# Attention's product with v does two or three steps in some slots and none in their neighbours

## The chip, the core and the metric

The kernel runs on one core of a Trainium2 chip. The core has five engines that take their instructions in order, each from its own list: TensorE (PE: matrix products and transposes, with PEld for the loads of its stationary operand), VectorE (DVE), ScalarE (ACT), GpSimd (POOL) and SyncE (SP, which issues the DMA transfers). They wait for one another on semaphores. The metric is the device time of one execution in microseconds (us).

## What is computed

Three stages follow one another, all on inputs in fp32 (the weights of the second arrive as 64-bit numbers):

```
q_assign = argmax(q_n . c_n); k_assign = argmax(k_n . c_n)     # 16 clusters
scores = where(q_assign == k_assign, q k^T / sqrt(64), -1e9)
attn = softmax(scores);  x = attn v                            # 2 x 8 heads, 768 rows, 64 wide
h = x w_in;  g = P(h) / Q(h);  x = g w_out                     # 1536 x 512, 2048 wide
out = soft mixture of 8 experts with 4 slots each (phi, w1, w2)
```

The change lies in the last product of attention, attn v.

## The kernel before

**Attention** works on pairs of heads: 8 pairs, and each pair in two halves of 384 query rows, so 16 half pairs. A half pair has 6 slots, one for each of 3 blocks of 128 query rows and 2 heads; there are 96 slots in all (NSL). The loop at L673 records slot after slot, and in this stage PE, ACT, DVE and POOL keep the order in which they are recorded (a manual schedule; SP too up to slot 12). In slot n:

- PE turns the exponentials of slot n, six transposes of 128x128 into the PSUM tile sT (`turn`, L413); ACT copies them out to eT (`turned`, L419).
- PE makes the scores of slot n+2: four products into the PSUM tile s (`a1_mm`, L389 and L390). DVE copies them out negated with their row minimum (`a1_neg`, L398, with a short instruction behind it that reads the minimum), and one slot later ACT takes the exponential (`a1_exp`, L402).
- PE does one step of the product with v of the half pair before (`a2_av`, L426). A half pair's product has six steps, one for each block j of 128 keys, summed up in the PSUM tile av; a step has a product for each of the two heads, which lie in two column halves of the array. One product of the kernel is two rows in the profile.
- Other work is planned into slots by name. On PE these are products with the centroids (L242), transposes (L263, L290, L447, L586, L607), products that make the masks (L312, L325), and products of the decoded weights with phi (L595). Work of kind P stands before the step with v, work of kind T behind it. On DVE the planned work of a slot stands before that slot's L398, and on ACT L549, L590 and others stand behind L419. Much of it decodes the 64-bit weights (`decode_steps`), and its DMAs go out on SP.

Of the tile s there is one buffer, so the scores of the next slot begin when L398 has read those before; of sT there is one, too, so a slot's transposes wait for the copy of the slot before. Of eT there are two: the half pair that is being filled, and the one that the product with v reads. All six blocks of a half pair are in eT when its product begins, six slots after its first transposes. The tile av is single; DVE reads it out in the first slot of the next half pair (`a2_x`, L466).

**The expert stages.** From slot 95 on, the loop at L964 makes 47 units of the second stage (four products L800, four L801, four L803 and then transposes L847, or products L859, each unit), in which PE and SP have a written order, while a list scheduler places the instructions of ACT, DVE and POOL. The 1 MB weight tiles of the last stage (`freed`, L780) are loaded in an order that follows PE's progress. The end of the program (from L982) is written out by hand.

Of the kernel before, what the change touches and what calls it, by code (L numbers as in the profile page):

```python
# [58 lines left out]
def tile_kernel(ctx, tc, qT, kT, v, cenT, cenP, consts, constsb, ab, w_in, w_out, phi, w1, w2, out, dbg=None):  # L59
# [77 lines left out]
    def load(p, names="kq"):  # L137
        b, hp = divmod(p, H // 2)
        r = raws.setdefault(p, {})
        for n in names:  # L140
            r[n] = raw_p.tile([128, S], F32, tag="raw" + n, name="raw" + n, bufs=2)
            SP.dma_start(r[n], (kT if n == "k" else qT)[b, hp])

    def load_v(p):
        b, hp = divmod(p, H // 2)
        vs[p] = v_p.tile([128, 2, 6, D], F32, tag="v", name="vt")
        SP.dma_start(vs[p], v[p])
# [232 lines left out]
    def a1_mm(u):  # L380
        p, idx = divmod(u, 12)
        half, rest = divmod(idx, 6)
        i, h = divmod(rest, 2)
        o = ops[p % NBUF][h]
        it = slice((3 * half + i) * 128, (3 * half + i + 1) * 128)
        ps = s1s[u] = psS[u == 1].tile([128, 2, 512], F32, tag="S", name="s1")
        for c in range(2):
            w = slice(c * HS, (c + 1) * HS)
            PE.matmul(ps[:, c, 0:HS], o["q1"][:, it], o["k1"][:, w], start=True, stop=False)  # L389
            PE.matmul(ps[:, c, 0:HS], o["q2"][0:80, it], o["k2"][0:80, w], start=False, stop=True)  # L390

    def a1_neg(u):
        g, rest = divmod(u, 6)
        if rest == 0:
            nvs[g] = s2_p.tile([128, 6], F32, tag="nv", name="nv", bufs=3)
            sums[g] = s2_p.tile([128, 6], F32, tag="ssum", name="ssum", bufs=3)
        e = es[u] = e_p.tile([128, 2, HS], F32, tag="e", name="e", bufs=3)
        DVE.tensor_scalar(e, s1s.pop(u)[:, :, 0:HS], -1.0, None, ALU.mult, ALU.min, accum_out=nvs[g][:, rest:rest + 1])  # L398

    def a1_exp(u):  # L400
        g, rest = divmod(u, 6)
        ACT.activation(es[u], es[u], AF.Exp, scale=-1.0, bias=nvs[g][:, rest:rest + 1], accum_out=sums[g][:, rest:rest + 1])  # L402
# [3 lines left out]
    def turn(u):  # L406
        g, rest = divmod(u, 6)
        if rest == 0:
            eTs[g] = e_p.tile([128, 2, 6, HS], F32, tag="eT", name="eT", bufs=2)
        e = es.pop(u).rearrange("p c (j t) -> p (c j) t", j=3)  # L410
        ps = eTp[u] = psS[1].tile([128, 2, 512], F32, tag="S", name="sT")
        for j in range(6):
            PE.transpose(ps[:, j // 3, j % 3 * 128:(j % 3 + 1) * 128], e[:, j, :], ident)  # L413

    def turned(u):
        g, rest = divmod(u, 6)
        i, h = divmod(rest, 2)
        dst = eTs[g][:, h, :, i * 128:(i + 1) * 128].rearrange("p (c j) t -> p c j t", c=2)
        ACT.copy(dst, eTp.pop(u)[:, :, 0:HS].rearrange("p c (j t) -> p c j t", j=3))  # L419

    def a2_av(g, js):
        if js[0] == 0:
            av[g] = psA.tile([128, 512], F32, tag="av", name="av")
        for j in js:
            for h in range(2):
                PE.matmul(av[g][64 * h:64 * h + 64, 0:HS], vs[g // 2][:, h, j, :], eTs[g][:, h, j, :],  # L426
                          start=(j == 0), stop=(j == 5))
# [29 lines left out]
    def a2_x(g):  # L457

        p, half = divmod(g, 2)
        b, c = divmod(p, H // 2)  # L460
        t0 = b * S + half * HS
        hold = {}

        def scale():
            hold["x"] = s2_p.tile([128, HS], F32, tag="x", name="x", bufs=1)
            DVE.tensor_tensor(hold["x"], av.pop(g)[:, 0:HS], Rs.pop(g), ALU.mult)  # L466

        def split():
            done = 0
            while done < HS:  # L470
                t, off = divmod(t0 + done, TB)
                n = min(HS - done, TB - off)
                src = hold["x"][:, done:done + n]
                dh, dl = xh[t][:, c, off:off + n], xl[t][:, c, off:off + n]
                POOL.tensor_scalar(dh, src, 1.0, 1.0, ALU.mult, ALU.mult)
                POOL.tensor_tensor(dl, src, dh.bitcast(F32), ALU.subtract)
                done += n

        return [(0, "D0", scale), (1, "G", split)]
# [11 lines left out]
    def idle(n):  # L491
        for _ in range(n):
            PE.matmul(rest_ps, zero[:, 0:128], zero, start=True, stop=True)
# [135 lines left out]
    def open_w():  # L629
        pctx.close()  # L630
        keep = ctx.enter_context(tc.tile_pool(name="keep", bufs=1, reuse_waits="tile"))
        return keep, bctx.enter_context(tc.tile_pool(name="wsp", bufs=2 * WAHEAD + 1, reuse_waits="tile"))

    def w_load(n):
        for a in range(2):
            wsp[n, a] = w_p.tile([128, NCC, 128], F32R, tag="w", name="w")
            SP.dma_start(wsp[n, a].rearrange("p c n -> p (c n)").bitcast(F32),
                         w_in2[n % NF][:, a].rearrange("p c n -> p (c n)"))


    NSL = 12 * NP
    plan = {}

    def add(slot, steps):
        for off, eng, fn in steps:
            plan.setdefault(slot + off, {}).setdefault(eng, []).append(fn)

    def run(slot, engines):
        for eng in engines:
            for fn in plan.get(slot, {}).pop(eng, []):  # L650
                fn()
# [10 lines left out]
    front, back, rest = prep(0)  # L662
# [9 lines left out]
    pend = None  # L672
    for n in range(-LEAD, NSL + 6):  # L673
        p, k = divmod(n, 12)
        if n == SP_FREE:
            manual.__exit__(None, None, None)
            manual = tc.manual_schedule(engines=engines)
            manual.__enter__()
        if n == -LEAD:
            run(-1, ("S",))  # L680
        if n == 0:
            run(1, ("S",))
            load_v(0)
            load(2, "k")
        if n == 1:
            load(2, "q")
        if n == 2:
            load_v(1)
        if k == 4 and n > 0 and p + 2 < NP:
            add(n, prep(p + 2))  # L690
        if k == 6 and 0 < p < NP - 1:
            load_v(p + 1)
        if n > 0 and k == 0 and p + 2 < NP and p:
            load(p + 2, "q")
        if n > 0 and k == 1 and p + 2 < NP and p:
            load(p + 2, "k")
        if n == NSL - OPENW:
            keep, w_p = open_w()
            for i in range(WAHEAD):
                w_load(i)  # L700
        g, rest = divmod(n - 6, 6)
        if 0 < g < 2 * NP and rest == 0:
            add(n, a2_x(g - 1))
        if n == NSL + 4:
            add(n, a2_x(g))
        if n == NSL - 8:
            DVE.tensor_scalar(ncoef, coef, -1.0, None, ALU.mult)
            DVE.tensor_tensor(babs, coef[:, 4:6], ncoef[:, 4:6], ALU.max)
        run(n, ("D0", "D", "D1", "D2", "G0", "S", "G"))
        if 0 <= n < NSL:  # L710
            turn(n)
        if pend is not None:
            a1_exp(pend)
            pend = None
        if 0 <= n < NSL:
            turned(n)
        run(n, "A")
        if n + LEAD < NSL:
            pend = n + LEAD
            if n > 0 or n == -LEAD:  # L720
                a1_mm(pend)
            a1_neg(pend)
            if n < 0:

                a1_mm(n + 1 + LEAD)
        run(n, "P")
        if n >= NSL:
            if n < NSL + 2:
                a2_av(g, range(3 * rest, 3 * rest + 3))
        elif g >= 0:  # L730
            a2_av(g, (rest,))
        run(n, "T")
        if n < 6 and n != -1:
            idle(2 if n < 0 else 3)
# [250 lines left out]
    n = nunit - 1  # L985
# [393 lines left out]
```

## Time and profile before

| | us |
|---|---|
| median of three runs | 536.92 |
| the three runs | 535.67, 536.92, 540.62 |
| the profiled execution, whole | 534.87 |
| its span in the trace | 533.1 |

Attention's slots 6 to 94 and the second stage's units take up most of the span: slot 6 begins at 35.67 us, slot 95 at 287.31 us, and the units run up to about 470 us. The mean granted clock of TensorE was 0.996 of full speed. In the profile's views a row that gives PE's matrix work as busy is modelled at its end, since products are pipelined: the distances between starts of rows tell what a piece of work costs the engine, and the length of a row does not. A piece of idle time is followed, in square brackets, by what ended it.

### The profile page before, as it was taken

To read this page: it belongs to the slowest core of one execution; us is meant where nothing else is said; L and a number is where in the kernel's file an instruction comes from. 1 tells how busy PE (TensorE), PEld (TensorE's weight loads), DVE (VectorE), ACT (ScalarE), POOL (GpSimd) and SP (SyncE) were. 2 spreads that over 40 slices of the span, in tenths; PEclk is the share of its full clock that TensorE was granted. 3 is DMA by queue.
4 is the path that set the end of the run, shared out by engine and by line. 5 is a ranking of instruction groups with operands and counts; after the bars stand their busy time and mean duration, and the time that the engine had idled before them with its cause. 6 is when DMAs were issued, how large, how long until landed. Compare 5 with 4: busy or idle time off the path is not lost.

```text
span 533.1 us, 10150 instructions
## 1 busy us (share of the span) xinstructions
PE 516.3 (97%) x3549; PEld 339.6 (64%) x3549; DVE 412.9 (77%) x800; ACT 382.3 (72%) x697; POOL 279.2 (52%) x322
## 2 busy tenths in 40 slices
PE   8989999999999999999999999999999999999994
PEld 3556656666576665665666677777677777765362
DVE  4798889888798798888742599999889996986022
ACT  2787888879878888697875598887688785872111
POOL 3444777367656777576622565565455554561000
PEclk9999999999999999999999999999999999999998
DMA  8698879597768876776530486676476674889997
GB/s 230 199 252 263 255 205 269 179 259 199 247 183 253 256 220 209 208 197 183 162 119 23 128 305 245 222 260 252 140 284 222 225 249 162 314 315 398 417 417 306
DMA packets 43571, 125.72 MB, mean 236 GB/s; under 512 B 6464, under 2 KB 7872, under 8 KB 38912
## 3 DMA queue, kind: packets, MB, share of 16 engines
q1 hardware_dynamic: 43376, 124.81, 71.5%
q8 instruction: 28, 0.46, 0.4%
q10 hardware_dynamic: 144, 0.26, 0.1%
q14 instruction: 23, 0.19, 0.1%
HBM read 89.66 MB, written 15.73 MB: 198 GB/s over the span
## 4 chain that ended last, share of the span: by engine, by line
PE 74%; DVE 14%; ACT 6%; DMA 4%; issue 2%; POOL 0%; DVEq 0%; ACTq 0%; POOLq 0%
PE av L426 10%; PE sT L413 10%; PE h L800 9%; PE h L803 8%; PE h L801 8%; PE s L389 4%; DVE e L398 4%; PE s L390 4%; DMA wt<-w 4%; PE gt L847 4%; PE pf L1212 3%; PE mf L242 2%; PE l L859 2%; ACT eT L419 2%; ACT e L402 2%
## 5 line engine op out<-in xcount | busy, mean ns | idle before, releaser
L398 DVE TENSOR_SCALAR_CACHE_REDUCE e<-s 128x768 f32<-128x768 f32 x96 | 91.5, 954 | 36.5 <-PE s L390 29.0
L402 ACT ACTIVATE e<-e,nv 128x768 f32<-128x768 f32 x96 | 89.9, 937 | 40.5 <-DVE e L398 33.5
L413 PEld LDWEIGHTS sT<-cst,e 128*128 128x128 f32 x576 | 61.4, 140 | 51.4 <-ACT eT L419 17.5
L413 PE MATMUL sT<-cst,e 128*128 128x128 f32 x576 | 83.8, 282 | 1.0 <-ACT eT L419 0.6
L419 ACT COPY eT<-sT 128x768 f32<-128x768 f32 x96 | 75.8, 789 | 10.2 <-PE sT L413 9.1
L426 PE MATMUL av<-eT,vt 128*64 128x384 f32 x384 | 82.0, 510 | 0.0
L800 PE MATMUL h<-xh,w 128*128 128x512 f32 x192 | 80.6, 420 | 0.0
L561 POOL TENSOR_TENSOR w<-mh,ex 128x516 f32<-128x516 f32 x32 | 42.4, 1325 | 65.3 <-DVE ex L556 34.2
L389 PE MATMUL s<-k,q 128*128 128x384 f32 x192 | 73.2, 381 | 2.9 <-DVE e L398 2.5
L801 PE MATMUL h<-xl,w 128*128 128x512 f32 x192 | 75.3, 392 | 0.0
L817 POOL TENSOR_SCALAR q<-u,babs 128x512 f32<-128x512 f32 x47 | 36.4, 774 | 73.3 <-ACT u L815 73.3
L390 PE MATMUL s<-k,q 80*128 80x384 f32 x192 | 64.9, 338 | 0.0
L819 POOL TENSOR_TENSOR q<-q,u 128x512 f32<-128x512 f32 x47 | 61.0, 1298 | 3.8
L803 PE MATMUL h<-xh,w 128*128 128x512 f32 x192 | 53.0, 396 | 0.0
L815 ACT ACTIVATE u<-h 128x512 f32<-128x512 f32 x47 | 27.9, 595 | 27.9 <-PE h L803 25.0
L800 PEld LDWEIGHTS h<-xh,w 128*128 128x128 f32 x192 | 36.1, 188 | 16.2 <-DVE p L832 4.2
L818 DVE TENSOR_TENSOR p<-p,h 128x512 f32<-128x512 f32 x47 | 32.1, 683 | 14.5 <-ACT p L816 14.4
L803 PEld LDWEIGHTS h<-xh,w 128*128 128x128 f32 x192 | 36.1, 188 | 8.6
L801 PEld LDWEIGHTS h<-xl,w 128*128 128x128 f32 x192 | 36.2, 189 | 6.7 <-issue 0.5
L389 PEld LDWEIGHTS s<-k,q 128*128 128x128 f32 x192 | 36.4, 190 | 6.1 <-DVE e L398 4.5
L825 ACT ACTIVATE r<-q,epsc 128x512 f32<-128x512 f32 x47 | 32.8, 698 | 8.1 <-POOL q L819 6.7
L390 PEld LDWEIGHTS s<-k,q 80*128 80x128 f32 x192 | 36.6, 191 | 0.1
(215 smaller groups left out, 994.5 us busy)
## 6 DMA issues: line engine op xcount, KB each, us to landing
wt<-w SPq DMA_DIRECT2D x32, 1024.0 KB, 8.0
w<-w_in SPq DMA_DIRECT2D x96, 256.0 KB, 3.2
raw<-w_in SPq DMA_DIRECT2D x16, 512.0 KB, 5.4
raw<-w_out SPq DMA_DIRECT2D x16, 512.0 KB, 4.4
w_in<-w SPq DMA_DIRECT2D x16, 512.0 KB, 3.4
k<-ka SPq DMA_DIRECT2D x32, 192.0 KB, 3.5
q<-qh SPq DMA_DIRECT2D x28, 192.0 KB, 4.4
w_out<-w SPq DMA_DIRECT2D x16, 256.0 KB, 3.8
```

Source lines behind the costliest of these rows:

```text
L389: PE.matmul(ps[:, c, 0:HS], o["q1"][:, it], o["k1"][:, w], start=True, stop=False)
L390: PE.matmul(ps[:, c, 0:HS], o["q2"][0:80, it], o["k2"][0:80, w], start=False, stop=True)
L398: DVE.tensor_scalar(e, s1s.pop(u)[:, :, 0:HS], -1.0, None, ALU.mult, ALU.min, accum_out=nvs[g][:, rest:rest + 1])
L402: ACT.activation(es[u], es[u], AF.Exp, scale=-1.0, bias=nvs[g][:, rest:rest + 1], accum_out=sums[g][:, rest:rest + 1])
L413: PE.transpose(ps[:, j // 3, j % 3 * 128:(j % 3 + 1) * 128], e[:, j, :], ident)
L419: ACT.copy(dst, eTp.pop(u)[:, :, 0:HS].rearrange("p c (j t) -> p c j t", j=3))
L426: PE.matmul(av[g][64 * h:64 * h + 64, 0:HS], vs[g // 2][:, h, j, :], eTs[g][:, h, j, :], start=(j == 0), stop=(j == 5))
L561: POOL.tensor_tensor(w.rearrange("p (r n) -> p r n", r=3), hold["mh"].bitcast(F32), hold["ex"].bitcast(F32), ALU.mult)
L800: PE.matmul(h, wh[:, c, :], xh[t][:, c, :], start=(c == 0), stop=False)
L801: PE.matmul(h, wh[:, c, :], xl[t][:, c, :], start=False, stop=False)
L803: PE.matmul(h, wl[:, c, :], xh[t][:, c, :], start=False, stop=(c == NCC - 1))
L819: POOL.tensor_tensor(q, q, u, ALU.mult)
```

## The change

A table AV of 90 digits says how many steps with v each of the slots 6 to 95 does. Its six digits for a half pair add up to six. `a2_av` takes the run of steps that are next in line, and takes its PSUM tile in the slot that has step 0.

```diff
@@ a2_av
-        if js[0] == 0:
+        if 0 in js:
             av[g] = psA.tile([128, 512], F32, tag="av", name="av")
@@ before the plan
     NSL = 12 * NP
+    AV = [int(c) for c in
+          "201111111201102021120201102201"
+          "111102111021121101012201112101"
+          "020211120201301101112101101112"]
     plan = {}
@@ the loop over slots
         elif g >= 0:
-            a2_av(g, (rest,))
+            done = sum(AV[6 * g:n - 6])
+            a2_av(g, range(done, done + AV[n - 6]))
         run(n, "T")
```

In 22 slots the digit is 0, in 20 it is 2, in slot 78 it is 3, and in the others 1. The slots with 0 are 7, 16, 19, 21, 26, 28, 31, 34, 40, 45, 52, 54, 58, 64, 66, 68, 74, 76, 79, 82, 88 and 91. Nothing else of attention moves on any engine or queue: the lists of ACT, DVE, POOL and SP up to the end of attention are the same.

On PE, slots 45 and 46, from the last product of slot 45's scores; a row `L426 ... x2` is one step with v (two products), L413 opens slot 46. Before:

```order
L390 MATMUL s_1984<-k_1_1_132,q_1_1_130 128x384
L586 MATMUL mf<-cst,w 128x128 x4
L426 MATMUL av<-eT,vt 64x384 x2
L413 MATMUL sT<-cst,e 128x128 x6
L389 MATMUL s_2012<-k_0_0_119,q_0_0_117 128x384
L390 MATMUL s_2012<-k_0_0_120,q_0_0_118 128x384
L389 MATMUL s_2012<-k_0_0_119,q_0_0_117 128x384
L390 MATMUL s_2012<-k_0_0_120,q_0_0_118 128x384
L447 MATMUL mf<-cst,rb 128x128 x3
L426 MATMUL av<-eT,vt 64x384 x2
```

And with the change:

```order
L390 MATMUL s_1984<-k_1_1_132,q_1_1_130 128x384
L586 MATMUL mf<-cst,w 128x128 x4
L413 MATMUL sT<-cst,e 128x128 x6
L389 MATMUL s_2010<-k_0_0_119,q_0_0_117 128x384
L390 MATMUL s_2010<-k_0_0_120,q_0_0_118 128x384
L389 MATMUL s_2010<-k_0_0_119,q_0_0_117 128x384
L390 MATMUL s_2010<-k_0_0_120,q_0_0_118 128x384
L447 MATMUL mf<-cst,rb 128x128 x3
L426 MATMUL av<-eT,vt 64x384 x4
```

The step has left the place between two sets of transposes and stands behind the step of slot 46.

On PE, slots 78 and 79, from the last product of slot 78's scores; L595 are products with phi in a quarter of the array's columns. Before:

```order
L390 MATMUL s_3176<-k_0_0_120,q_0_0_118 128x384
L426 MATMUL av<-eT,vt 64x384 x2
L413 MATMUL sT<-cst,e 128x128 x6
L389 MATMUL s_3210<-k_0_1_123,q_0_1_121 128x384
L390 MATMUL s_3210<-k_0_1_124,q_0_1_122 128x384
L389 MATMUL s_3210<-k_0_1_123,q_0_1_121 128x384
L390 MATMUL s_3210<-k_0_1_124,q_0_1_122 128x384
L426 MATMUL av<-eT,vt 64x384 x2
L595 MATMUL mf<-wT,ph 32x128 x4
```

And with the change:

```order
L390 MATMUL s_3176<-k_0_0_120,q_0_0_118 128x384
L426 MATMUL av<-eT,vt 64x384 x6
L413 MATMUL sT<-cst,e 128x128 x6
L389 MATMUL s_3214<-k_0_1_123,q_0_1_121 128x384
L390 MATMUL s_3214<-k_0_1_124,q_0_1_122 128x384
L389 MATMUL s_3214<-k_0_1_123,q_0_1_121 128x384
L390 MATMUL s_3214<-k_0_1_124,q_0_1_122 128x384
L595 MATMUL mf<-wT,ph 32x128 x4
```

Three steps now stand ahead of slot 79's transposes and scores, and between its scores and L595 there is none.

Behind attention, PE's list differs by one product (the last half pair's remaining steps stand one L803 earlier), and the list scheduler places the same instructions of ACT and DVE in another order for some twelve units of the second stage's first block (L818, L820 and L832 to L834 on DVE, L815 to L826 and L850 on ACT).

## Rows read from the trace of the kernel before

**Rows 1.** The page: span, busy time and share of each engine, chain by engine.

```profile
span 533.1 us, 10150 instructions
PE 516.3 (97%) x3549; PEld 339.6 (64%) x3549; DVE 412.9 (77%) x800; ACT 382.3 (72%) x697; POOL 279.2 (52%) x322
PE 74%; DVE 14%; ACT 6%; DMA 4%; issue 2%; POOL 0%; DVEq 0%; ACTq 0%; POOLq 0%
```

**Rows 2.** Windows, busy us by engine, clock, DMA: slots 6 to 94, and units.

```profile
35.67:287.31 251.64, 246.28 (x1672) 156.81 (x1671) 206.15 (x424) 205.58 (x377) 155.13 (x180) 1.00 0.72 209
303.89:469.00 165.11, 165.11 (x872) 123.30 (x871) 151.18 (x246) 130.60 (x231) 93.01 (x90) 1.00 0.67 239
```

**Rows 3.** Timeline of PE, slots 82 to 84: start us, length us, instruction.

```profile
256.05 0.34 PE L390 MATMUL s<-k,q 80*128 80x384 f32 x1
256.22 0.49 PE L447 MATMUL mf<-cst,rb 128*128 128x128 f32 x3
256.55 0.60 PE L586 MATMUL mf<-cst,w 128*128 128x128 f32 x4
257.08 0.87 PE L426 MATMUL av<-eT,vt 128*64 128x384 f32 x4
257.88 0.87 PE L413 MATMUL sT<-cst,e 128*128 128x128 f32 x6
258.51 0.42 PE L389 MATMUL s<-k,q 128*128 128x384 f32 x1
...
259.12 0.33 PE L390 MATMUL s<-k,q 80*128 80x384 f32 x1
259.38 0.87 PE L426 MATMUL av<-eT,vt 128*64 128x384 f32 x4
...
261.69 0.87 PE L426 MATMUL av<-eT,vt 128*64 128x384 f32 x4
262.49 0.42 PE L595 MATMUL mf<-wT,ph 128*32 128x128 f32 x8
```

**Rows 4.** Timeline of PE behind slot 95: six steps with v in a row.

```profile
294.46 4.09 PE L426 MATMUL av<-eT,vt 128*64 128x384 f32 x24
298.48 0.55 PE L447 MATMUL mf<-cst,rb 128*128 128x128 f32 x3
```

**Rows 5.** Timeline of PE, slot 1, whose transposes follow a product of full width.

```profile
22.05 0.82 PE L413 MATMUL sT<-cst,e 128*128 128x128 f32 x6
22.62 0.42 PE L389 MATMUL s<-k,q 128*128 128x384 f32 x1
```

**Rows 6.** Timeline of PE, slot 40: a mask product and the step behind it.

```profile
136.53 0.32 PE L325 MATMUL mf<-oT,W 80*128 80x384 bf16 x1 [0.70 <-ACT nh L317]
136.78 0.87 PE L426 MATMUL av<-eT,vt 128*64 128x384 f32 x4
```

**Rows 7.** Timeline of DVE, slots 83 and 34: L398 and its reader.

```profile
259.49 0.96 DVE L398 TENSOR_SCALAR_CACHE_REDUCE e<-s 128x768 f32<-128x768 f32 x1 [1.25 <-PE s L390]
260.37 0.09 DVE L398 DVE_READ_ACCUMULATOR e<-s 128x1 f32 x1
118.38 0.07 DVE L398 DVE_READ_ACCUMULATOR e<-s 128x1 f32 x1
```

**Rows 8.** Timeline of PE, slots 34 and 79: scores that waited.

```profile
116.98 0.87 PE L413 MATMUL sT<-cst,e 128*128 128x128 f32 x6
118.51 0.44 PE L389 MATMUL s<-k,q 128*128 128x384 f32 x1 [0.65 <-DVE e L398]
246.47 0.87 PE L413 MATMUL sT<-cst,e 128*128 128x128 f32 x6
248.14 0.44 PE L389 MATMUL s<-k,q 128*128 128x384 f32 x1 [0.79 <-DVE e L398]
```

**Rows 9.** Waits of PE's loads, slots 6 to 94: total us, times, longest.

```profile
PEld s L389 <- DVE e L398: 3.7, 6, 1.0
```

**Rows 10.** Waits of SP's queue from 298 us on.

```profile
SPq L637 <- PE h L801: 102.5, 44, 6.5
```

## Prediction, made before the changed kernel ran

> **What bounds the kernel now.** I read the page first. PE is busy 97% of the span and holds 74% of the chain that ended last, DVE 14%, ACT 6% [rows 1]. Such a PE row is modelled at its end, so I went on to the windows: in slots 6 to 94 PE is busy 246 of 251.64 us, DVE 206, ACT 206, at the full clock [rows 2]. That is 2.83 us a slot (251.64/89), against 2.32 us of DVE and 2.31 us of ACT work. Then I read PE's timeline by the distances between starts, which tell what a piece costs. The reader is to see two things there: the same piece costs more beside work of another width, and in few places PE waits at all.
>
> **The price of a step.** A step alone takes 0.80 us from its start to the next transposes (257.08 to 257.88) or to L595 (261.69 to 262.49) [rows 3]. Six in a row take 4.02 us (294.46 to 298.48) [rows 4], so a step behind another takes (4.02 - 0.80)/5 = 0.644 us. Each of the 22 moved steps is now behind another: 0.156 us less.
>
> The way into a step costs as well. Three transposes L447 take 0.33 us up to the next transposes, 0.11 each, but four L586 take 0.53 up to the step: 0.09 more than 0.44. From the last score product it is 0.26 us to a step (259.12 to 259.38) and 0.17 to a transpose (256.05 to 256.22): 0.09 again [rows 3]. And the way out: transposes behind a step need 0.63 us up to the scores (257.88 to 258.51) [rows 3], behind a full-width product 0.57 [rows 5], 0.06 less. Where the emptied slot's step stood behind a mask product L325, its way in is 0.25 [rows 6]; I have no clean row for L325 straight into transposes, bound it by 0.11 (as between transposes) and 0.25, and take 0.25, since the mask product is of another type and 384 columns long. So nothing is saved on that way in; the other end would add 6 x 0.14 = 0.84.
>
> The 22 emptied slots, by what stands round the step:
> - six (19, 34, 45, 82, 88, 91) with transposes or scores ahead and sT behind: 0.156 + 0.09 + 0.06 = 0.306 each, 1.84;
> - six (16, 28, 40, 52, 64, 76) with L325 ahead and sT behind: 0.156 + 0.06 = 0.216 each, 1.30;
> - ten (7, 21, 26, 31, 54, 58, 66, 68, 74, 79) with narrow products L242 or L595 behind. These use a part of the columns themselves, so I let them keep the dear way in: 0.156 each, 1.56.
>
> Sum: PE has **4.7 us** less to do.
>
> **Waits that are filled.** In slot 34 the scores start 1.53 us after the transposes instead of 0.63, in slot 79 1.67: 0.90 and 1.04 us of PE waiting for DVE's L398 of the slot before [rows 8]. Slot 33 now does two steps and 78 three. DVE works through its backlog meanwhile, so min(0.90, 0.64) + min(1.04, 1.29) = 1.7 us go. All six such waits sum to 3.7 us [rows 9]. I take 2.7, half way, as I have not looked whether each of the other four follows a fuller slot.
>
> **Waits that are new.** With one buffer for s there is a loop: scores start to L398 start 0.98 us (258.51 to 259.49), L398 and its reader 0.97 (to 260.46), 0.06 from there to the next scores (118.45 to 118.51) [rows 3, 7, 8]. So scores cannot follow scores faster than 2.01 us. In an emptied slot PE itself needs 0.61 + 0.17 for the scores, its other work, and 0.57 for the transposes [rows 3, 5]. With three transposes between (slot 34) that is 1.68, 0.33 short of the loop; with four (45, 91) 1.79, 0.22 short each; with L447 and L325 (16, 28, 52, 64, 76) 0.33 + 0.25 give 1.93, 0.08 short each; with L595 alone (21, 79: its row is 0.42 long) some 0.1 each. Sum 1.4 us, the lower bound. The upper: 18.9 us (14.2 for the steps at 0.644, and the 4.7) over 22 slots is 0.86 less in each, and a mean slot of 2.83 would come to 1.97; if each has to hold the mean DVE work of 2.32 all the same, 22 x 0.35 = 7.7 us. The emptied slots hold more other PE work than the mean slot, DVE runs over slot borders, and it sat idle 1.25 us before the L398 of slot 83 [rows 7], so I take 2.9, nearer to the lower end.
>
> **The same sum by a rule.** PE's loads of stationary operands are busy 156.81 of 251.64 us there, 62% [rows 2]. The Trainium skill (Perfetto Trace Analysis, Identifying the Most-Contended Engine) holds that matmul busy time is no good measure of how near TensorE is to its limit and goes by the share of weight loads instead. By that, PE has over a third in hand, and the terms above would be worth nothing. The trace agrees on the first half: a row of L447 x3 is 0.49 us long, its cost 0.33 [rows 3]. It does not on the second, as far as I read it: the distances are those of PE's own pace where no wait is shown. I keep it as a rival.
>
> **What stays of it.** Every later piece follows PE: the 47 units run with PE busy 165.11 of 165.11 us [rows 2], and SP's queue waits on PE's products for 102.5 us in 44 places [rows 10], so the loads come earlier with it; DMA is at 0.67 there and is not what would hold them. What attention gives therefore reaches the end. The new order of ACT and DVE in twelve units I price at nothing: DVE has 151.18 of 165.11 us of work, so PE covers it; without that cover a unit that waits for one DVE instruction loses about 151.18/246 = 0.6 us.
>
> **Sum.** -4.7 - 2.7 + 2.9 = -4.5 us. The profiled execution took 534.87 us (its span 533.1 and 1.8 around it) and would take 530.4; it lies 2.05 under the median of the three runs, so against the median the forecast is 536.92 - 4.5 = **532.4 us**. The ends of the terms: -4.7 - 3.7 + 1.4 = -7.0 (529.9) and -4.7 - 1.7 + 7.7 = +1.3 (538.2).
>
> **Rivals.**
> - *DVE catches up and PE is fuller than I charge* (0.27). All six waits go, the new ones stay near the loop's 1.4: -7.0, 529.9 us. For it: the idle 1.25 us of DVE; 20 slots in which it has 0.64 us more. Against: DVE is at 82% in attention, and its work does not shrink where PE's does. The case begins at -5.4.
> - *PE is not what sets the slots* (0.17). Then emptied slots wait for DVE or ACT as much as they gain, the upper end of the new waits: +1.3, 538.2 us. The case holds all from there down to -2.8. The skill's rule on weight loads would come out here. For it: DVE and ACT each have 2.3 us of work against some 2.0 of PE's in an emptied slot. Against: 74% of the chain on PE.
> - *Slower* (0.06). The fuller slots surely pay 22 x 0.644 = 14.2 us; the emptied ones should return 18.9. If the loop of scores and L398 (or the copy of sT) holds them nearly at their old length, less comes back. The point is 14.2 - 5.4 = 8.8 us: if the emptied slots return less than that, under half, the kernel is slower by over 1%. At 5 returned it takes 546 us. For it: one buffer each of s and sT. Against: the loop of 2.01 us is shorter than nearly all emptied slots are now.
> - That the change does not do what it says is out: PE's order shows the moved rows, and no other list changes in attention.
>
> **How the numbers follow.** The forecast has a chance of 0.50. 1%, or 5.4 us, is about what a measurement of this kernel can tell from no change. The forecast's range runs from -2.8 to -5.4 us, so it counts as within 1%, as does the second rival: 0.67 in all. The first rival is faster by over 1%: 0.27. The last is slower: 0.06. The range of 8 in 10 holds the forecast, most of the first rival and most of the second: 529.8 to 536.6 us.
>
> **What would show it.** In the changed profile: rows L426 x8 with 1.44 us to the next start (1.60 if steps don't join up); the transposes of slot 83 0.44 us behind L586's start in place of 1.33 [rows 3]; the scores of slots 34 and 79 without most of their wait; new waits of L389 for L398 behind slots 34, 45 and 91; slot 95 begins 5.1 us sooner (it does two steps itself); the units unchanged at 165 us. The prediction is wrong if L389's waits in attention sum to well over 4 us, if steps in a row cost 0.80 each, or if the gain of attention is lost again in the units.

## The result and the profile after

The changed kernel takes 530.73 us (median of 13 runs, 528.48 to 536.09) against 536.95 us for the kernel before (13 runs, 535.66 to 540.62). The ratio, of the means and not of the medians, is 0.9892, with a 95% interval of 0.9861 to 0.9923: 5.8 us faster, 4.1 to 7.5. A second series of the same kernel (below) gave 531.67 us and 0.9904 (0.9866 to 0.9942), 5.2 us faster, 3.1 to 7.2. The forecast was 4.5 us, in a range of 529.8 to 536.6 us.

The profiled execution took 530.71 us, about the median; that of the kernel before took 534.87 us, 2.1 under the median of its 13 runs, so it is a quick one. Behind line 642 the line numbers have moved by 4 or 5 (L800 is L805, L801 is L806, L803 is L808). The page of the changed kernel, span and busy time:

```profile
span 528.8 us, 10145 instructions
PE 512.2 (97%) x3546; PEld 342.3 (65%) x3549; DVE 413.7 (78%) x800; ACT 381.2 (72%) x697; POOL 277.0 (52%) x322
```

The windows of the changed kernel (start and end, length, then busy us of PE, PEld, DVE, ACT, POOL, clock, DMA share, GB/s), for slots 6 to 94 and for the 47 units:

```profile
35.74:281.30 245.56, 241.88 (x1668) 159.05 (x1666) 207.27 (x424) 204.01 (x377) 153.27 (x180) 1.00 0.72 214
298.52:463.63 165.11, 165.11 (x872) 123.35 (x871) 150.75 (x246) 130.91 (x231) 92.64 (x90) 1.00 0.66 239
```

Beside [rows 2], attention is 6.08 us shorter (245.56 for 251.64) and the units are the same to the last digit, 165.11 us. DVE and ACT have the work that they had (207 and 204 us for 206 and 206). What got shorter is PE.

PE's timeline of the changed kernel, at slots 10, 33 to 35, 78 to 79 and 82 to 83 (start, length, instruction, and the idle time ahead with what ended it):

```profile
47.80 0.87 PE L413 MATMUL sT<-cst,e 128*128 128x128 f32 x6
48.64 0.41 PE L389 MATMUL s<-k,q 128*128 128x384 f32 x1
49.39 0.45 PE L390 MATMUL s<-k,q 80*128 80x384 f32 x1 [0.34 <-DMA q<-qh]
...
115.35 1.51 PE L426 MATMUL av<-eT,vt 128*64 128x384 f32 x8
116.79 0.88 PE L413 MATMUL sT<-cst,e 128*128 128x128 f32 x6
117.42 0.42 PE L389 MATMUL s<-k,q 128*128 128x384 f32 x1
...
118.21 0.49 PE L447 MATMUL mf<-cst,rb 128*128 128x128 f32 x3
119.01 0.87 PE L413 MATMUL sT<-cst,e 128*128 128x128 f32 x6 [0.30 <-ACT eT L419]
...
241.59 2.16 PE L426 MATMUL av<-eT,vt 128*64 128x384 f32 x12
243.68 0.88 PE L413 MATMUL sT<-cst,e 128*128 128x128 f32 x6
244.31 0.42 PE L389 MATMUL s<-k,q 128*128 128x384 f32 x1
...
252.29 0.60 PE L586 MATMUL mf<-cst,w 128*128 128x128 f32 x4
252.73 0.83 PE L413 MATMUL sT<-cst,e 128*128 128x128 f32 x6
```

- Two steps take 1.44 us to the next start (115.35 to 116.79) and three 2.09 (241.59 to 243.68): 0.80 and 0.644 for each one behind it, the price of [rows 4].
- Behind the four L586 the transposes of slot 83 start after 0.44 us; before, the step and they took 1.33 [rows 3].
- The scores of slots 34 and 79 start 0.63 us after their transposes (116.79 to 117.42, 243.68 to 244.31): the waits of 0.90 and 1.04 us are gone [rows 8].
- Two rows show waits that were not there. In slot 10 the scores stand for a load of q (48.64 to 49.39 for a distance that is 0.26 elsewhere). Behind slot 34 it is the transposes that wait, for ACT's copy of the tile sT: 0.80 us from L447 where its own pace is 0.33.

The waits in attention, of PE's weight loads (first row, against [rows 9]) and of PE, and the wait of SP's queue in the units (against [rows 10]):

```profile
PEld s L389 <- DVE e L398: 2.1, 7, 0.6
```

```profile
PE sT L413 <- ACT eT L419: 0.7, 3, 0.3
PE s L389 <- DVE e L398: 0.5, 2, 0.3
PE s L390 <- DMA q<-qh: 0.3, 1, 0.3
```

```profile
SPq L637 <- PE h L806: 102.2, 44, 6.5
```

To split the 6.0 us, I took each distance between starts of PE's rows of two kinds, subtracted the distance that this pair of kinds has where nothing waits, and called the rest a wait. The slot lengths then fall into PE's own work and its waits. "Unit 2" is the start of the first unit behind the last steps with v (299.09 us before). A pair of rows that never stands undisturbed counts as work, so the split is good to some tenths.

| profile | slot 6 starts | slots 6 to 94 | own work | waits | slot 95 to unit 2 | unit 2 to the last unit | from there to the last load of L780 | span |
|---|---|---|---|---|---|---|---|---|
| before | 35.67 | 251.64 | 243.01 | 8.63 | 11.78 | 166.74 | 58.50 | 533.1 |
| changed | 35.74 | 245.56 | 237.50 | 8.07 | 12.42 | 166.75 | 59.62 | 528.8 |
| changed, once more | 36.10 | 246.76 | 237.54 | 9.22 | 12.42 | 166.76 | 59.37 | 530.1 |

PE's own work in slots 6 to 94 fell by 5.51 us. Of this 0.64 is a step that has only moved on: slot 95 does two now. Up to unit 2 PE therefore has 4.87 us less to do. Its waits fell by 0.56 net in the first profile, while in the second they are 0.59 more than before. So the units begin 5.36 us sooner in the first profile and 3.8 in the second. Each unit keeps these 5.36 us (465.84 against 460.48 at the last).

### The profile page after: what moved, and what is told of

It is laid out like the page before. It is cut to its first block, busy times and chain, and to the rows that moved or that the text cites. A ratio compares the mean times of both kernels' runs of the same rounds, so it can differ in the third digit from the quotient of the medians.

```text
span 528.8 us, 10145 instructions
## 1 busy us (share of the span) xinstructions
PE 512.2 (97%) x3546; PEld 342.3 (65%) x3549; DVE 413.7 (78%) x800; ACT 381.2 (72%) x697; POOL 277.0 (52%) x322
## 4 chain that ended last, share of the span: by engine, by line
PE 43%; DMA 7%; DVE 2%; ACT 1%; issue 1%; DVEq 0%; SPq 0%
PE h L805 9%; PE h L808 8%; PE h L806 8%; DMA wt<-w 7%; PE gt L852 4%; PE av L426 3%; PE sT L413 2%; PE l L864 2%; PE dg L926 1%; PE s L389 1%; PE s L390 1%; PE dg L1144 1%; PE pw L1179 1%; ACT e L402 0%; DVE e L398 0%
## 5 line engine op out<-in xcount | busy, mean ns | idle before, releaser
L398 DVE TENSOR_SCALAR_CACHE_REDUCE e<-s 128x768 f32<-128x768 f32 x96 | 91.4, 953 | 29.4 <-PE s L390 26.5
L413 PEld LDWEIGHTS sT<-cst,e 128*128 128x128 f32 x576 | 61.9, 140 | 46.5 <-ACT eT L419 17.0
L413 PE MATMUL sT<-cst,e 128*128 128x128 f32 x576 | 83.3, 281 | 1.0 <-ACT eT L419 0.7
L805 PE MATMUL h<-xh,w 128*128 128x512 f32 x192 | 80.6, 420 | 0.0
L426 PE MATMUL av<-eT,vt 128*64 128x384 f32 x384 | 77.2, 504 | 0.0
L806 PE MATMUL h<-xl,w 128*128 128x512 f32 x192 | 75.3, 392 | 0.0
L389 PE MATMUL s<-k,q 128*128 128x384 f32 x192 | 73.3, 382 | 1.2 <-DVE e L398 0.8
L808 PE MATMUL h<-xh,w 128*128 128x512 f32 x192 | 52.9, 396 | 0.0
L820 ACT ACTIVATE u<-h 128x512 f32<-128x512 f32 x47 | 28.0, 595 | 27.4 <-PE h L808 23.8
L805 PEld LDWEIGHTS h<-xh,w 128*128 128x128 f32 x192 | 36.1, 188 | 16.2 <-DVE r L838 3.4
L808 PEld LDWEIGHTS h<-xh,w 128*128 128x128 f32 x192 | 36.0, 188 | 8.6
L806 PEld LDWEIGHTS h<-xl,w 128*128 128x128 f32 x192 | 36.2, 189 | 6.7 <-issue 0.5
L389 PEld LDWEIGHTS s<-k,q 128*128 128x128 f32 x192 | 36.4, 189 | 4.9 <-DVE e L398 2.8
```

What stands on the lines that cost most here:

```text
L805: PE.matmul(h, wh[:, c, :], xh[t][:, c, :], start=(c == 0), stop=False)
L806: PE.matmul(h, wh[:, c, :], xl[t][:, c, :], start=False, stop=False)
L808: PE.matmul(h, wl[:, c, :], xh[t][:, c, :], start=False, stop=(c == NCC - 1))
```

## The experiments

**Steps in the same slots, but not side by side.** In the 13 fuller slots that have P work, one step is done ahead of it and the rest behind it.

```diff
+        ahead = 0
+        if 6 <= n < NSL and AV[n - 6] > 1 and plan.get(n, {}).get("P"):
+            done = sum(AV[6 * g:n - 6])
+            a2_av(g, (done,))
+            ahead = 1
         run(n, "P")
...
-            a2_av(g, range(done, done + AV[n - 6]))
+            a2_av(g, range(done + ahead, done + AV[n - 6]))
```

> The changed kernel with the same table, but in 13 of the fuller slots (6, 15, 20, 22, 27, 32, 41, 46, 56, 62, 67, 69, 75) one of the two steps stands ahead of the slot's planned work on PE and the other behind it, so that they do not follow each other. Theory (the gain is mostly PE work saved where steps join up and where widths change less often): PE's own work comes back by 0.156 + 0.09 + 0.06 = 0.3 us in eight slots with transposes between and some 0.25 in five with a mask product, 3.7 us in all, so slot 95 begins near 285.0 us instead of 281.3, and the time is some 3.7 us over the changed kernel's. Rival (the gain is the evening out of crowded and light slots, and joining steps is worth nothing): the same number of steps in each slot, so slot 95 begins at 281.3 again.

It took 533.81 us, ratio to the kernel before 0.9960 (0.9929 to 0.9992). PE's own work rose by 3.46 us against the changed kernel (expected 3.7), its waits were 7.60 us, and slot 95 began at 284.17 us. PE's timeline, slot 22:

```profile
83.47 0.87 PE L426 MATMUL av<-eT,vt 128*64 128x384 f32 x4
84.26 0.55 PE L447 MATMUL mf<-cst,rb 128*128 128x128 f32 x3
84.74 0.87 PE L426 MATMUL av<-eT,vt 128*64 128x384 f32 x4
85.53 0.87 PE L413 MATMUL sT<-cst,e 128*128 128x128 f32 x6
```

Both steps pay the single price again, 0.79 us each (83.47 to 84.26, 84.74 to 85.53), and three transposes between them 0.48 in place of 0.33. By the ratios 0.68 of the 1.08% hang on steps that stand side by side, or 0.56 of the 0.96% by the second series: 3.0 to 3.7 us, as the 3.46 of PE's work say.

**Only the six moves in front of scores that waited.** Steps move only out of slots 26, 34, 52, 58, 64 and 79.

```diff
-          "201111111201102021120201102201"
-          "111102111021121101012201112101"
-          "020211120201301101112101101112"]
+          "111111111111111111120111111201"
+          "111111111111121101111201112101"
+          "111111111111201111111111111111"]
```

> Only six of the 22 moves: the steps of slots 26, 34, 52, 58, 64 and 79 go to fuller slots ahead of a place where PE waited before. Theory: own work falls by 1.4 us (three at 0.156, one at 0.306, two at 0.30), waits by some 1.9, so slot 95 begins near 284.0 us (3.3 before the kernel before's 287.3). Rival (filled waits are the whole gain): nearly all of the 6.0 us that the changed kernel gains up to slot 95, so 281.5 to 282.

**The other sixteen moves.**

```diff
+          "201111111201102021111201102111"
+          "111102111021111111012111111111"
+          "020211120201211101112101101112"]
```

> The other 16 moves alone (without the steps of slots 26, 34, 52, 58, 64, 79). No fuller slot stands ahead of one of the large waits. Theory: own work falls by 4.1 us up to slot 95, new waits give back some 1.3, so slot 95 begins near 284.5 us, 2.8 sooner than before. Rival (filled waits are the whole gain): no sooner than before, 287.3, or later by the new waits, 288.5.

The first took 534.08 us (0.9945, 0.9917 to 0.9974), the second 533.29 us (0.9934, 0.9905 to 0.9964). PE's own work fell by 1.28 and 4.17 us, as the prices said (1.4 and 4.1), and the two add up to the 5.51 of the whole change within 0.1. The waits did not come as expected: the six moves took away 0.52 us net where I expected 1.9, and the sixteen added 2.92 where I expected 1.3. But the profile with the sixteen moves is of an execution of 535.76 us, 2.5 over that kernel's median, and its new waits are mostly for loads: 1.8 us stand in slot 10, where a step had moved ahead and q came late, and 1.2 in slots 24 and 25, behind a load of raw weights for which DVE stood 1.45 us in front of L545. PE's waits in attention with the sixteen moves, and that one of DVE:

```profile
PE s L389 <- DVE e L398: 1.5, 4, 0.7
PE s L389 <- DMA q<-ql: 1.0, 1, 1.0
...
PE s L390 <- DMA q<-qh: 0.4, 1, 0.4
```

```profile
DVE ex L545 <- DMA raw<-w_in: 1.5, 1, 1.5
```

The times of the two halves do add up: 0.55 and 0.66% make 1.21, against 1.08 and 0.96% for the whole change, within the intervals. That the waits of the halves do not add up is thus not shown.

**Every second slot empty, the next does two.** The digits are 02, 45 times over.

```diff
+          "020202020202020202020202020202"
+          "020202020202020202020202020202"
+          "020202020202020202020202020202"]
```

> The table is 020202 throughout: 45 slots with two steps, 45 with none. Theory: own work up to slot 95 falls by some 10 us (0.22 a step by the changed kernel's 22 moves), but an emptied slot has 1.87 us of PE work on average, 0.14 under the loop of scores and L398 and 0.45 under DVE's mean work, so waits come to 6 to 20 us and slot 95 begins between 284 and 297 us; the sum of waits for L398 in PE's rows is far over the 2 us of the changed kernel. Rival (joining is everything, waits stay as they are): slot 95 near 277 us.

It took 543.26 us, ratio 1.0122 (1.0091 to 1.0152): slower than before. PE's own work is the least of all, about 8.8 us below the kernel before, but its waits came to about 26.1 us, 17.5 more (here the split is rougher, by up to 1 us, as some pairs of rows hardly occur undisturbed). PE's waits, and its timeline at a place where a mask product now stands straight ahead of transposes:

```profile
PE sT L413 <- ACT eT L419: 4.5, 13, 0.7
PE s L389 <- DVE e L398: 3.7, 7, 1.3
PE s L389 <- DVE mh L552: 2.2, 1, 2.2
```

```profile
103.29 0.33 PE L325 MATMUL mf<-oT,W 80*128 80x384 bf16 x1
103.46 0.82 PE L413 MATMUL sT<-cst,e 128*128 128x128 f32 x6
```

This is the rival "slower" of the prediction, reached with another table: with 45 emptied slots the scores and the transposes run into DVE and ACT. The changed kernel empties 22 slots and keeps its waits at 8 to 9.5 us. The two rows of the timeline also give the price that I had to bound: L325 to transposes is 0.17 us, not 0.25.

**Another table, the changed kernel once more, and the gain given back.** Three kernels on one chip. The second table empties 23 slots:

```diff
+          "100401211020102111121011001311"
+          "111201012111121101010401212010"
+          "010122111111301101111102111210"]
```

> Another table of the same kind (23 slots without a step; steps stand ahead of places where PE still waits in the changed kernel: slot 39 does two so that the mask product of slot 40, which waits 0.87 us, comes later; slot 9 does four ahead of the scores of slot 10, which wait 0.81; slot 95 does none). By the prices of the steps PE's own work up to the second unit falls by 4.4 us against the kernel before, as much as in the changed kernel (4.5). So if only the joining counts, the time is that of the changed kernel, 530.7 us, and unit 2 starts at 293.7. If the waits that are left (8.1 us) can be placed away, up to 4 of them go: unit 2 between 290 and 292, whole 526.7 to 529. I expect half of it, 528.7; the waits did not add up in the two half tables, so a miss in waits is the likeliest way to fail.

> The changed kernel once more, on another chip perhaps, with a second profile. If the 1.1 us that its loads of the last stage lost against attention's gain belongs to the kernel (another order of work in the units, another place in memory), the second profile shows it again: slot 95 near 281.3, last landing near 520.1, whole 530.7. If it belongs to the single execution, attention is the same and the last landing comes at 518.9 to 519.5, or the loads lose elsewhere; the whole varies by about 1 us with the loads.

The third has 23 idle products in front of unit 2:

```diff
+        for _ in range(23 if n == 2 else 0):
+            PE.matmul(h, wh[:, 0, :], xh[t][:, 0, :], start=True, stop=True)
```

> The changed kernel with 23 extra products in front of unit 2's own (their result is overwritten; 0.233 us each by the starts of such rows: 5.36 us), which is what attention gained at that place: unit 2's own work then starts at 299.1 as in the kernel before. If what attention gives is carried to the end whole, the time is that of the kernel before: 536.9 us, ratio 1.000. If the changed order of ACT and DVE in the units costs something, or the last stage does, this kernel is slower than before by it: 538.0 for the 1.1 us. If loads and not PE set the end, the filler costs less than it is long: 533 to 535.

The other table took 531.03 us (0.9888, 0.9860 to 0.9916), the changed kernel 531.67 us (0.9904, 0.9866 to 0.9942), the one with the idle products 537.73 us (1.0012, 0.9990 to 1.0034). The idle products in PE's timeline:

```profile
295.07 5.53 PE L805 MATMUL h<-xh,w 128*128 128x512 f32 x23
300.44 0.39 PE L807 MATMUL h<-xh,w 128*128 128x512 f32 x1
```

They take 5.37 us (295.07 to 300.44) and cost 1.08% of 536.4, 5.8 us, uncertain by 2.4: all of what attention gained, and the kernel is back at the time of the one before (0.5 us less to 1.8 more). So what PE saves in attention reaches the end, and neither the new order of ACT and DVE in the units nor the last stage costs more than that. The 1.1 us that the first profile lost behind the units (58.50 to 59.62 in the table above) is not settled: it was there in the second profile (59.37), and not behind the idle products (58.01).

The other table did not gain the 2 us that I expected: unit 2 starts at 293.75 us, with waits of 8.05 us. Waits of 2.9 us were gone (slots 14, 17, 22, 27, 29, 46, 72, 92 and 94), and as much had come, most of it in slots 10, 11 and 53 (now 1.34, 0.52 and 1.16). The second profile of the changed kernel showed what comes there. DVE's timeline in slots 51 and 52, and PE's in slot 53:

```profile
168.02 0.08 DVE L398 DVE_READ_ACCUMULATOR e<-s 128x1 f32 x1
170.21 0.69 DVE L545 TENSOR_SCALAR ex<-raw 128x516 int32<-128x516 int32 x1 [2.10 <-DMA raw<-w_out]
170.81 0.68 DVE L546 TENSOR_SCALAR mh<-raw 128x516 int32<-128x516 int32 x1
171.41 0.95 DVE L398 TENSOR_SCALAR_CACHE_REDUCE e<-s 128x768 f32<-128x768 f32 x1
```

```profile
170.84 0.82 PE L413 MATMUL sT<-cst,e 128*128 128x128 f32 x6
172.42 0.44 PE L389 MATMUL s<-k,q 128*128 128x384 f32 x1 [0.76 <-DVE e L398]
```

A load of raw weights lands late; DVE stands 2.10 us in front of L545; L398 is queued behind it; the next scores wait for L398, 1.58 us behind the transposes in place of 0.63. In the first profile of the same kernel DVE waited 0.15 us there, and the scores of slot 53 did not wait. In the profile of the other table DVE's longest wait for such a load is 2.3 us, at the same place. The view names DVE as the one waited for, but the cause is a load.

**Half of each load of raw weights left out**, in the changed kernel and in the one before. The half of the tile that is not loaded holds zeros.

```diff
-        POOL.memset(t.rearrange("p r n t -> p (r n t)")[:, 1024:1032], 0)
+        POOL.memset(t.rearrange("p r n t -> p (r n t)")[:, 512:1032], 0)
...
-            SP.dma_start(raw.rearrange("p r n t -> p (r n t)")[:, 0:1024], src)
+            SP.dma_start(raw.rearrange("p r n t -> p (r n t)")[:, 0:512], src[:, 0:512])
```

> The changed kernel with half of each load of 64-bit weights left out (32 loads of 256 KB instead of 512; the other half of the tile holds zeros, so half of the decoded weights are wrong; no instruction is added or taken away on PE, ACT and DVE). Theory: attention's PE work is the same in every execution (237.5 us), and what varies, 8.07 us of PE's waits in one profile and 9.22 and 9.52 in two others, is loads that land late: DVE's L545 waits for one (0.4, 3.5 and 1.0 us), L398 stands behind it, and the scores wait for L398. Then PE's waits come to 7.5 or less, L545 waits for no load, slot 95 begins by 281.0, the time is 530.0 or less, and the runs lie closer together than from 528.5 to 536.1. Rival: the new waits are DVE's own work behind slots without a step; then waits of 8 to 9.5 us, slot 95 at 281.3 to 282.9, and 530.7 to 531.7 us.

> The kernel before with the same half of each load of 64-bit weights left out. Theory: slots that take longer leave the loads time enough, so the kernel before gains less by it than the changed one: L545's one wait of 1.1 us goes, PE's waits stay at 8.2 to 8.6, slot 95 at 287.0 to 287.3, 536.4 to 536.9 us. Rival: it gains as much as the changed kernel or more; then late loads are not a thing of the change, and its gain is not held by them.

They took 529.65 us (0.9873, 0.9847 to 0.9898; runs from 526.57 to 531.81) and 535.61 us (0.9984, 0.9968 to 0.9999). L545 waited for no load in either, and in the changed kernel the waits of L389 in slots 50 and 53 were gone. But my numbers failed: the profile of the first has 9.7 us of waits, not 7.5 or less, and slot 95 at 282.82; that of the second 9.24 us, and 288.13. In the first 3.6 us stand in slots 10 and 11: 2.1 in slot 10's scores, for q again (a load of q lands at 49.44 us, the scores start at 49.58), the rest behind them, which I did not follow. Outside these two slots 6.1 are left, less than the 7.3, 8.7 and 9.2 us of the other profiles of this order. By the medians the kernel before gains 0.8 us and the changed one 1.1 to 2.0. The first is hardly clear of noise, and the interval of the second overlaps those of both series without the edit. So what late loads of weights cost is not settled, and nothing shows that they are a thing of the change alone.

**The load ahead of q's moved behind it.** Slot 10 has one load of 384 KB in front of those that it needs; with SP_FREE, the slot up to which SP's order is written by hand, at 13 it goes behind them.

```diff
-    SP_FREE = 12
+    SP_FREE = 13
```

> The changed kernel with one load (rawq of a later pair, 384 KB) moved behind the six loads q<-qh and q<-ql that slot 10's scores need; a few instructions of DVE and POOL in slots 12 and 13 change places with it. In nine profiles the third of those loads lands between 48.7 and 50.6 us, and slot 10's scores wait for it by 0.37 to 2.58 us in the changed kernels, by 0.09 in the kernel before. Theory: what slots 6 to 9 save ends in that wait. Then the load lands 0.7 to 1 us earlier, slot 10's wait falls below 0.4 us, and slot 95 begins 0.4 to 1.5 us earlier than with the same loads behind it, at 280.2 to 281.3; whole 529.5 to 530.7. Rival: the load's issue, which follows POOL, or the wait of PE for DVE sets slot 10; then its wait stays at 0.4 to 0.8, and the time at 530.7 to 531.7.

> The kernel before with the same load moved. Its scores of slot 10 wait for the load by 0.09 us only where the load lands early, so by the theory it gains less than the changed kernel: 0 to 0.3 us where the load lands as in its first profile, slot 95 at 287.0 to 287.3, 536.6 to 536.9 us. Rival: it gains as much as the changed kernel, or the reordered instructions of slots 12 and 13 cost something, which then shows in both.

> The other table of the fifth experiment with the same load moved. There slots 10 and 11 waited 1.86 us for q. If the load is what they wait for, most of it goes: unit 2 at 292.2 to 293, 528.5 to 530 us, the fastest of all. If not, 531.0 as before.

The changed kernel with it took 531.53 us (0.9886, 0.9855 to 0.9916), the kernel before with it 537.15 us (1.0005, 0.9982 to 1.0028), the other table with it 529.37 us (0.9856, 0.9825 to 0.9886). Slot 10's wait for q went in all three, from 0.81 and 0.48 us to 0.02 in the changed kernel and, with slot 11's, from 1.86 to nothing with the other table. In the changed kernel it brought no time: the instructions of slots 12 and 13 that change places with the load cost 0.65 us in slot 13, and the kernel before has the same 0.64 there. PE's timeline of the changed kernel with it:

```profile
49.07 0.87 PE L413 MATMUL sT<-cst,e 128*128 128x128 f32 x6
49.70 0.42 PE L389 MATMUL s<-k,q 128*128 128x384 f32 x1
49.96 0.36 PE L390 MATMUL s<-k,q 80*128 80x384 f32 x1
...
56.99 0.87 PE L413 MATMUL sT<-cst,e 128*128 128x128 f32 x6
58.27 0.44 PE L389 MATMUL s<-k,q 128*128 128x384 f32 x1 [0.41 <-DVE e L398]
```

In slot 10 the second score product follows after 0.26 us (49.70 to 49.96), its own pace. In slot 13 the scores come 1.28 us behind the transposes, where 0.63 is their pace. With the other table slot 13 does not wait, and that kernel has the lowest median of all. Its unit 2 starts at 293.64 us and not by 293 (slot 6 starts 0.6 us later than with this table before, and slot 53 waits 1.76 us for a load of raw weights). Its interval overlaps that of the changed kernel, so that it is faster, by the 0.3 to 0.5% of the ratios, is not shown.

## Why the prediction came out as it did

The forecast was 4.5 us less; the two series gave 5.8 and 5.2. By the forecast's own bounds that is at the border of the first rival (from 5.4), and just over or just under the 1% that it counted as no change; both intervals hold 4.5. The first rival itself did not come: it wanted new waits near 1.4 us, and there are 3.1.

- **The price of a step: right.** 0.80 and 0.644 us show in the rows after, and the split steps show that the price comes from standing side by side.
- **The sum of 4.7 us of PE work: right to 0.2 us, with errors in it that partly cancel.** The 5.51 us of slots 6 to 94 hold the 0.64 of the step that went to slot 95; 4.87 is what stands against 4.7. For the six slots with a mask product L325 ahead I took the way into transposes as 0.25 us, the dear one of two bounds, and wrote that nothing is saved there. It is 0.17, so each saves 0.08 to 0.09, 0.5 us in all, and this is the term that was mis-sized. The other sixteen slots gave some 0.3 us less than the 3.4 forecast for them, spread over many distances that I did not trace. That the two nearly cancel is luck. The product's type and length, on which I chose the bound, were no guide. Its rows are 80*128 like the transposes' 128*128, where a step's are 128*64; that the width alone sets the price was not tried.
- **Waits that are filled: 2.7 taken, 3.6 measured** (first profile, slot by slot, of all kinds), near the end of 3.7. The two that I had worked out went whole; slots 34 and 79 have shorter waits for the copy of sT in their place (0.47 and 0.32), taken off the 3.6, which I had put into the slower rival alone.
- **Waits that are new: 2.9 taken, 3.1 measured, but not all of the kind that I priced.** Behind eight emptied slots (16, 21, 26, 28, 45, 64, 76 and 91) the scores wait 1.7 us for L398, near the lower end of 1.4. But 0.7 us stand in slot 10 for a load, and 0.3 in slot 50. The prediction looked at loads only in the units, and wrote that DMA would not hold them. In attention the waits differ from execution to execution: 8.07, 9.22 and 9.52 us in three profiles of the same order, own work within 0.04. The places where they differ most are ones that stand for loads, in slots 10 and 59 for q and in slot 53 for raw weights. Net of what is filled, the forecast took 0.2 us more waits; against the one profile before, the three show 0.56 less, 0.59 more and 0.89 more.
- **Slot 95: 5.1 us sooner forecast; 6.0, 4.4 and 4.7 in the three profiles.** The forecast lies among them; the 6.0 of the first is 0.2 of PE's work and 0.8 of waits more than forecast.
- **What stays of it: right.** The units took 165.11 us again and the idle products gave the gain back.
- **The rival that PE does not set the slots: wrong here.** By the Trainium skill (Perfetto Trace Analysis, Identifying the Most-Contended Engine) the weight loads' 62% would have left PE a third in hand (MFU, the share of peak arithmetic that the page names beside it, I did not work out). The whole change took 5.8 and 5.2 us off the time and 4.87 off PE's work, the sixteen moves 3.5 and 3.5 (their 4.17 hold the 0.64 of slot 95, too), and the split steps gave 3.46 back for 3.0 to 3.7. The six moves took off 2.9 us (1.4 to 4.5) for 1.28 of work and 0.52 of waits. The weight loads' share rose to 65% (159.05 of 245.56).
- **The slower rival: its mechanism is real, its point was far.** The digits 02 throughout reach it (1.22%, 0.91 to 1.52).

## What to carry to other kernels

Price PE's work by distances between starts, one price for each pair of neighbours: the same products cost less side by side (0.644 for 0.80 us here), and a sum over such pairs came out additive in halves of the change, within 0.1 us. When work moves over the border of the stretch that is measured, take it out of the sum before it is compared with the forecast. Waits are less firm: they differed by 1.5 us between executions of one order, so price them as a net sum with a wide range, do not read a tenth of a per cent from one profile, and for each place that comes earlier look up the landing of the load that it reads, not only the engine that it waits for. To learn whether a gain is carried to the end, give it back as idle work at one place and see whether the old time returns.

## What was not expected of the hardware

- The same loads take longer in one execution than in another. The view of tile q from 30 to 53 us, issue to landing of its loads (least, median, most), in the changed kernel (its second profile has 3.8 as the median) and then with the sixteen moves, another kernel but with the same loads in the same order:

```profile
DMA to landing us min/median/max: 3.7/4.2/4.6
```

```profile
DMA to landing us min/median/max: 3.9/5.1/5.7
```

  In the kernel before the load that slot 10 needs landed at 49.03 us and was read at 49.09: a load with nothing to spare, in a profile that shows no wait for it.
- The program's start varies as well: slot 6 begins between 35.31 and 37.02 us in the fourteen profiles, and from the last unit to the last load it takes 58.0 to 59.6 us. With attention's 1.5 us these come to 4 or 5 us, while the 13 runs of the changed kernel lie 7.6 us apart; what makes up the rest of the spread is not known.
